# A ring of five 4 KB cells in place of seven, value loads in single cells, and two more resident rows of wq

## The chip, the cores and the metric

One core of one Trainium2 chip. The time is the device time of one execution in microseconds; a kernel's runs are compared with runs of the kernel before taken in the same rounds on the same chip. Lower is better. The sets of runs were taken on different chips; where two kernels of different sets are compared by their medians below, the difference by their ratios is the same within 4 us.

PE is the engine of the matmuls, DVE, ACT and POOL are the vector, scalar and GpSimd engines, and SP is the engine whose queue issues all loads. A load *lands* when the last of its 16 completion increments has come.

## The reference, cut to what matters

A decode step of two layers. Both layers use the same weights and the same key and value cache.

```python
B, Sq, D = 8, 1, 512; Hq, Hkv, Sk, Dh = 32, 8, 8192, 128; F = 1792      # bfloat16
for layer in range(2):
    x = x + attention(layernorm(x), k_cache, v_cache, wq, wo)    # softmax(q k^T * Dh**-0.5) v, then wo
    x = x + silu(layernorm(x) @ w1) @ w2
```

The cache is 134 MB of keys and 134 MB of values. Keys are read once and serve both layers, values are read once for each layer: in all 134 + 268 MB, and with them 38 MB of wo, 21 MB of wq and 4 MB of FFN weights.

## The kernel before

A small planner in the program, run when it is built, replays an estimated timetable of loads and engine work. It fixes the order of instructions on every engine and the cell that each load goes to. All loads stand in one queue (SP), in one order. Keys have eight slots of their own. Values, wo tiles and the rows of the second half of wq share a ring of cells of 4 KB a partition (512 KB a cell); a load waits until PE has read what its cell held before.

```python
N_CELL = 7
class Plan:
    PE_SLOW = 1.15                         # factor on the estimates of PE's work
    @staticmethod
    def place(free, cells):                # which cell: a lone free one for one cell, two side by side for a pair
        ...
def values(h, wo=None, cells=2):           # one unit: one batch, one KV head, one layer
    for P in range(4):                     # four quarters of the values
        if P == (2 if cells == 2 else 3) and wo is not None:
            h["wo"] = load_wo(wo)          # layer 0 only: its wo tile, ahead of the unit's last value load
        if P % cells == 0:
            vn = load_v(b, g, P, cells)
        def pv(P=P, vn=vn): ...            # 8 matmuls read the cell
        n = plan.add(f"v{u}.{P}", "PE", 0.35, pv, pr, [h["exp"], vn, old or clear_n] + vs[-1:])
        if P % cells == cells - 1:
            frees(n, vn)                   # only now may the cells be loaded again
    ...                                    # gather, spread, multiply by wo: only then is the wo cell free
def queries_1(tag, prio, b0, nb, deps):    # heads 16 to 31
    for kt in range(KT):                   # four rows of the second half of wq, through the ring, for every batch
        wn = load_wq(1, kt)
        ...
```

The batches go through in passes. A pass takes in eight keys and the values that go with them (the *mixed stretch*), then a run of values and wo tiles without keys (the *value-only stretch*), then the FFN and the next pass.

Of the kernel before, what the change touches and what calls it, by code (L numbers as in the profile page):

```python
# [8 lines left out]
DH = 128  # L9
SM_SCALE = DH ** -0.5  # L10
LN_EPS = 1e-5

N_CELL = 7
N_SC = 3
N_P = 3
N_DEF = 4
# [119 lines left out]
class Plan:  # L136
# [3 lines left out]
    RATE = {1: 2.57, 2: 2.51, 4: 2.48}  # L140
    LAND = 2.0
    HOP = 0.1
    PE_SLOW = 1.15

    def __init__(self):
        self.nodes = []
# [104 lines left out]
def _build(ctx, nc, A_x, A_k_cache, A_v_cache, A_wq, A_wo, B_w1, B_w2, out):  # L251
# [9 lines left out]
    GR = SLOT // 4  # L261
# [5 lines left out]
    def sb(shape, dt, name):  # L267
        return ctx.enter_context(nc.sbuf_tensor(name, shape, dt))
# [4 lines left out]
    ring = sb([128, N_CELL * GR], BF16, "ring")  # L273
    kts = sb([128, G * SLOT], BF16, "kts")
    wq0 = sb([128, KT, GR], BF16, "wq0")
    w1_sb = sb([128, KT, F], BF16, "w1")
    w2_sb = sb([128, FT, D], BF16, "w2")
    ident = sb([128, 128], BF16, "ident")
# [38 lines left out]
    syn = Sync(nc, ctx)  # L317
    ksem = [DmaCounter(syn.new_sem(f"kt{i}")) for i in range(G)]
    rsem = [DmaCounter(syn.new_sem(f"ring{i}")) for i in range(N_CELL)]
    wsem = {n: DmaCounter(syn.new_sem(f"w_{n}")) for n in ("w1", "w2", "x", "wq0")}  # L320
    osem = syn.new_sem("osem")

    table = {}
# [331 lines left out]
    def queries_1(tag, prio, b0, nb, deps):  # L655

        qp = MI[:, 0:16 * nb]
        last = []
        for kt in range(KT):
            wn = load_wq(1, kt)  # L660

            def mul(kt=kt, wn=wn):
                steps = []
                for h in range(16):
                    steps.append(lambda h=h: pe.matmul(
                        qp[:, h * nb:(h + 1) * nb], gran(wn.give)[:, h * DH:(h + 1) * DH], xn[:, b0:b0 + nb, kt],
                        start=(kt == 0 and h == 0), stop=(kt == KT - 1), skip_group_check=True))
                mms(steps, reads=cells_of(wn) + [res("xn")], writes=[res("misc")], add=kt > 0)

            last = [plan.add(f"{tag}.r{kt}", "PE", 0.5, mul, prio, [wn] + deps + last)]  # L670
            frees(last[0], wn)
        n = plan.add(f"{tag}.qc4", "DVE", 0.17, lambda: query_copy(4, 8, qp, nb), prio, last)
        return {g: n for g in range(4, 8)}

# [23 lines left out]
    def keys(layer, b, g, q_dep, late=None, first=False):  # L698
# [39 lines left out]
        for q in range(4):  # L738
            def score(q=q):

                kv = slot(g).rearrange("p (c y i f) -> p y f c i", c=8, y=8, f=4)
                steps = []
                for y in range(2):
                    for t in range(4):
                        w = bd[:, 48 * q + 16 * (1 - y):48 * q + 16 * (1 - y) + 32]
                        steps.append(lambda t=t, y=y, w=w: pe.matmul(  # L746
                            sc[32 * t:32 * t + 32, 0:256], w, kv[:, 2 * t + y, q],
                            start=(q == 0 and y == 0), stop=(q == 3 and y == 1)))
                mms(steps, reads=[res("kt", g), res("bd", u % N_BD)], writes=[res(*scr)], add=(q > 0))
            sn.append(plan.add(f"s{u}.{q}", "PE", 0.3, score, pr - 1,  # L750
                               [tn[3], bn] + sn[-1:]))

        if layer == 1:
# [62 lines left out]
    ot_users = []  # L816
    es = []

    def values(h, wo=None, cells=2):

        layer, b, g, u, sm = h["layer"], h["b"], h["g"], h["u"], h["sm"]
        pr = count[0] - 1
        pt, o = ps[sm], len(ot_users) % N_OT
        ot = OT[o]
        hd = slice(R * g, R * g + R)
        old = back(ot_users, N_OT)
        vs = []
        for P in range(4):
            if P == (2 if cells == 2 else 3) and wo is not None:
                h["wo"] = load_wo(wo)  # L830
            if P % cells == 0:
                vn = load_v(b, g, P, cells)

            def pv(P=P, vn=vn):


                vt = gran(vn.give, cells).rearrange("p (a c t n) -> p a c t n", a=cells, c=2, t=4)[:, P % cells]
                steps = []
                for c in range(2):
                    for t in range(4):  # L840
                        k = 32 * (2 * P + c) + 8 * t
                        steps.append(lambda t=t, c=c, k=k: pe.matmul(  # L842
                            ot[32 * t:32 * t + 2 * R, 0:2 * DH], pt[:, k:k + 2 * R], vt[:, c, t],
                            start=(P == 0 and c == 0), stop=(P == 3 and c == 1)))
                mms(steps, reads=cells_of(vn) + [res("p", sm)], writes=[res("ot", o)], add=(P > 0))
            n = plan.add(f"v{u}.{P}", "PE", 0.35, pv, pr, [h["exp"], vn, old or clear_n] + vs[-1:])
            if P % cells == cells - 1:
                frees(n, vn)
            vs.append(n)

        def high():
            op(act, lambda: act.activation(pt[:, :], ot[:, 0:2 * DH], ACT.Copy), reads=[res("ot", o)],  # L852
               writes=[res("p", sm)])

        def low():
            op(dve, lambda: dve.tensor_tensor(part[:, :], ot[:, 0:2 * DH], pt[:, :], ALU.subtract),  # L856
               reads=[res("ot", o), res("p", sm)], writes=[res("part")])

        def gather():

            steps = []
            for k, src in enumerate((pt, part)):
                for y in range(2):
                    steps.append(lambda k=k, src=src, y=y: pe.matmul(  # L864
                        EX[:, 0:R], src[:, y * DH:y * DH + DH], diag[:, R * y:R * y + R],
                        start=(k == 0 and y == 0), stop=(k == 1 and y == 1)))
            mms(steps, reads=[res("p", sm), res("part"), res("diag")], writes=[res("ex")])

        hn = plan.add(f"hi{u}", "ACT", 0.42, high, pr - 2, [vs[-1]])
        ln = plan.add(f"lo{u}", "DVE", 0.45, low, pr - 2, [hn, back(es, 1)])  # L870
        es.append(plan.add(f"g{u}", "PE", 0.2, gather, pr - 2, [ln, back(ot_users, 1)]))
        if layer == 1:
            def norm():
                op(dve, lambda: dve.tensor_tensor(qab[:, b, hd], EX[:, 0:R], rcp[sm], ALU.mult),
                   reads=[res("ex"), res("rcp", sm)], writes=[res("attnb", g, b)])

            h["n"] = plan.add(f"n{u}", "DVE", 0.17, norm, pr - 2, [es[-1], h["rc"]])
        else:
            zt = zts[o]

            def cast():
                op(act, lambda: act.activation(attna[:, hd], EX[:, 0:R], ACT.Copy), reads=[res("ex")],
                   writes=[res("attna", g)])

            def spread():
                steps = [lambda j=j: pe.matmul(  # L886
                    EX[:, 8 + R * j:8 + R * j + R], sel[:, j].rearrange("p a k -> p (a k)"), attna[:, hd],
                    start=True, stop=True) for j in range(R)]
                mms(steps, reads=[res("sel"), res("attna", g)], writes=[res("ex")])

            def own():
                v = EX[:, 8:8 + R * R].rearrange("p (j h) -> p j h", h=R)
                op(dve, lambda: dve.tensor_tensor(  # L893
                    zt[:, :].rearrange("p (j h) -> p j h", h=R), v,
                    rcm[sm].unsqueeze(1).to_broadcast([128, R, R]), ALU.mult),
                    reads=[res("ex"), res("rcm", sm)], writes=[res("z", o)])

            n = plan.add(f"cast{u}", "ACT", 0.2, cast, pr - 2, [es[-1]])
            n = plan.add(f"spread{u}", "PE", 0.2, spread, pr - 2, [n])
            h["n"] = plan.add(f"own{u}", "DVE", 0.17, own, pr - 2, [n, h["rc"]])  # L900
            h["z"] = o
        ot_users.append(h["n"])
        p_users[sm] = [vs[-1], h["n"]]
# [39 lines left out]
    free_yt = [None]  # L943
    y_now = [None]

    def a_values(h, cells=2):
        values(h, wo=h["g"], cells=cells)
        y_now[0] = out_proj_a(h, y_now[0] if h["g"] else free_yt[0])

    ffn_deps = []  # L950
# [46 lines left out]
    for b in range(-1, NB):  # L997
        ready = None
        prio = FIRST
        if b >= 0:  # L1000
# [3 lines left out]
            ready = norm_nodes(f"c{b}.ln2", prio, b, 1, [n])  # L1004
            second_q.update(queries_0(f"c{b}", prio, b, 1, [ready]))
            for h in held:
                values(h, cells=1)
                ends.append(h)
        ks, vs, held_units = pass_of(b)
        made = {}  # L1010
# [2 lines left out]
        def advance(unit):  # L1013
            while unit not in made:
                k = todo.pop(0)
                layer, kb, g = k
                if layer == 0:
# [2 lines left out]
                        load_wq0()  # L1020
                        first_q.update(queries_0("f", FIRST, 0, NB, [f5]))
                    if kb == 0 and g == 4:
                        first_q.update(queries_1("f", count[0] - 5, 0, NB, [f5]))
                    made[k] = keys(0, kb, g, first_q[g])
                else:
                    if g == 4:
                        second_q.update(queries_1(f"c{b}", count[0] - 3, b, 1, [ready]))
                    made[k] = keys(1, kb, g, second_q[g], held_units.index(k) if k in held_units else None, g == 0)

        for i, v in enumerate(vs):  # L1030
# [1 line left out]
            if b == NB - 1 and i == 5:  # L1032
                load_wo_all()
            if v[0] == 0:
                a_values(made[v], cells=1 if b >= 0 and i >= len(vs) - 3 else 2)
            else:
                values(made[v], cells=1 if i < 2 else 2)
                ends.append(made[v])
        held = [made[k] for k in held_units]
        if b < 0:  # L1040
# [69 lines left out]
```

## Time and profile before

| | before |
|---|---|
| median time, first measurement | 1188.71 us (1183.99 to 1195.29, 3 runs) |
| bytes read from HBM | 465.05 MB |
| busy: PE, DVE, ACT, POOL | 60%, 51%, 12%, 10% |
| share of the chain that ended last that is DMA | 76% |

It is a kernel bound by the stream from HBM: no engine is near full, and the DMA engines are busy from end to end. The views that carry this are in the prediction. Two more are wanted later. The first has time windows of the kernel before over one value-only stretch and the mixed stretch that follows; after the window and its length come busy time and instructions of PE, PE's weight loads, DVE, ACT and POOL, then the granted clock, the DMA share and GB/s.

```profile
224.00:265.00 41.00, 28.87 (x580) 14.70 (x584) 13.01 (x42) 4.55 (x16) 2.50 (x6) 0.54 1.02 406
266.00:363.00 97.00, 56.64 (x1056) 29.37 (x1048) 60.12 (x168) 12.30 (x43) 11.64 (x29) 0.74 1.01 413
```

Both stretches run at the rate of a full queue. The second has the waits of the queue's sequencer, SP (total us, times, longest):

```profile
SPq L91 <- PE ot L842: 654.1, 300, 21.5
SPq L91 <- PE sc L746: 155.1, 29, 13.2
SPq L91 <- PE yt L915: 28.6, 17, 3.7
```

SP waits most of the time for PE to release a cell (ot is the values' product, yt the product with wo). That costs nothing as long as enough issued loads still stand in the DMA queue.

### The profile page before, as it was taken

What the parts mean: (1) busy time and instruction counts of PE and PEld (TensorE: products, weight loads), DVE (VectorE), ACT (ScalarE), POOL (GpSimd) and SP (SyncE); (2) the same over time, 40 slices, a digit from 0 to 9 for tenths busy, and PEclk for the clock granted to TensorE, in tenths of its full rate; (3) what the DMA queues carried; (4) which work ended last, traced back from release to release, by engine and by line L of the source; (5) the groups of instructions that cost most, each with busy time, mean ns of one, the idle gap of its engine ahead of it and who ended that gap; (6) DMA issues with size and microseconds to landing.
All of it is one profiled execution on the core that took longest, in us unless ns stands there. A gap on an engine that the chain in (4) does not pass through costs nothing.

```text
span 1180.7 us, 31675 instructions
## 1 busy us (share of the span) xinstructions
PE 706.9 (60%) x13588; PEld 370.5 (31%) x13588; DVE 597.7 (51%) x1713; ACT 136.9 (12%) x475; POOL 117.3 (10%) x295
## 2 busy tenths in 40 slices
PE   2544555675565755666665755667556575566844
PEld 1322332242332423323332323324233242333423
DVE  5652367625564255733667254752557336663321
ACT  0010011101111110110111111111101111111110
POOL 1000011101110010100111010110001001110110
PEclk9765677657676676756777568765667567675775
DMA  9999799999999999999999999999999999999993
GB/s 365 421 419 346 311 420 421 414 403 403 422 411 412 398 381 417 422 408 391 421 421 407 400 412 412 415 411 400 413 415 406 371 393 421 422 410 403 384 354 149
DMA packets 86413, 467.13 MB, mean 396 GB/s; under 512 B 8944, under 2 KB 14848, under 8 KB 61952
## 3 DMA queue, kind: packets, MB, share of 16 engines
q1 hardware_dynamic: 86272, 465.10, 97.8%
q8 instruction: 107, 1.75, 0.6%
q14 instruction: 34, 0.28, 0.1%
HBM read 465.05 MB, written 0.01 MB: 394 GB/s over the span
## 4 chain that ended last, share of the span: by engine, by line
DMA 76%; PE 16%; issue 4%; DVE 2%; SPq 1%; POOLq 0%; ACT 0%; POOL 0%; DVEq 0%; ACTq 0%
DMA ring<-in_A_v_cache_dram 70%; PE ot L842 7%; PE sc L746 6%; DMA kts<-in_A_k_cache_dram 3%; DMA ring<-in_A_wq_dram 2%; DMA w<-in_B_w_dram 1%; DVE kts L694 1%; PE misc L642 1%; SPq L340 1%; PE ex L864 0%; PE sc L721 0%; PE yt L915 0%; PE misc L510 0%; DVE small L758 0%; PE ex L886 0%
## 5 line engine op out<-in xcount | busy, mean ns | idle before, releaser
L842 PE MATMUL ot<-ring,p 128*8 128x256 bf16 x4096 | 256.6, 365 | 220.8 <-DMA ring<-in_A_v_cache_dram 218.9
L694 DVE STREAM_TRANSPOSE kts<-kts 128x1024 uint32<-128x1024 uint32 x256 | 306.1, 1222 | 35.4 <-DMA kts<-in_A_k_cache_dram 35.3
L746 PE MATMUL sc<-kts,bd 128*32 128x256 bf16 x4096 | 288.6, 406 | 33.8 <-DVE kts L694 21.7
L842 PEld LDWEIGHTS ot<-ring,p 128*8 128x8 bf16 x4096 | 80.0, 92 | 313.9 <-DMA ring<-in_A_v_cache_dram 288.7
L746 PEld LDWEIGHTS sc<-kts,bd 128*32 128x32 bf16 x4096 | 116.3, 117 | 107.4 <-DVE kts L694 32.1
L856 DVE TENSOR_TENSOR part<-ot,p 128x256 bf16<-128x256 f32 x128 | 54.2, 423 | 177.1 <-ACT p L852 98.5
L763 POOL PARTITION_ALL_REDUCE small<-small x128 | 47.8, 373 | 637.4 <-DVE small L759 383.1
L772 ACT ACTIVATE expd<-sc,small 128x256 bf16<-128x256 f32 x128 | 60.7, 474 | 422.1 <-DVE small L767 365.6
L852 ACT ACTIVATE p<-ot 128x256 bf16<-128x256 f32 x128 | 49.1, 383 | 487.7 <-PE ot L842 486.7
L778 PE MATMUL sc<-expd,ident 128*32 128x256 bf16 x512 | 42.3, 318 | 91.1 <-ACT expd L772 88.4
L758 DVE TENSOR_REDUCE small<-sc 128x1 f32<-128x256 f32 x128 | 53.2, 415 | 51.3 <-PE sc L746 51.2
L792 POOL PARTITION_ALL_REDUCE small<-small x128 | 55.3, 432 | 214.2 <-DVE small L788 214.2
L729 DVE TENSOR_TENSOR bd<-sc,mask 128x64 bf16<-128x64 f32 x128 | 27.7, 217 | 83.1 <-PE sc L746 73.9
L785 DVE STREAM_TRANSPOSE p<-sc 128x256 bf16<-128x256 bf16 x128 | 56.9, 445 | 7.3 <-PE sc L778 4.5
L778 PEld LDWEIGHTS sc<-expd,ident 128*32 128x32 bf16 x512 | 15.4, 109 | 121.9 <-ACT expd L772 119.5
L788 DVE TENSOR_SCALAR small<-hm,small 128x4 f32<-128x4 f32 x128 | 26.4, 206 | 33.4 <-ACT expd L772 33.4
L864 PE MATMUL ex<-diag,p 128*128 128x4 bf16 x256 | 26.3, 172 | 23.5 <-DVE part L856 21.2
L915 PE MATMUL yt<-z,ring 128*128 128x4 bf16 x1024 | 36.1, 166 | 6.1 <-DVE z L893 4.5
L915 PEld LDWEIGHTS yt<-z,ring 128*128 128x128 bf16 x1024 | 31.2, 100 | 27.0 <-issue 26.8
L864 PEld LDWEIGHTS ex<-diag,p 128*128 128x128 bf16 x256 | 16.4, 104 | 72.2 <-issue 38.5
L767 DVE SCALAR_TENSOR_TENSOR small<-small,hm 128x4 f32<-128x4 f32 x128 | 19.4, 152 | 37.4 <-POOL small L763 37.2
L759 DVE TENSOR_SCALAR small<-hneg,small 128x4 f32<-128x4 f32 x128 | 29.4, 230 | 4.5
(82 smaller groups left out, 433.9 us busy)
## 6 DMA issues: line engine op xcount, KB each, us to landing
ring<-in_A_v_cache_dram SPq DMA_DIRECT2D x260, 512.0 KB, 8.2
kts<-in_A_k_cache_dram SPq DMA_DIRECT2D x64, 2048.0 KB, 11.2
ring<-in_A_v_cache_dram SPq DMA_DIRECT2D x126, 1024.0 KB, 11.0
ring<-in_A_wo_dram SPq DMA_DIRECT2D x64, 512.0 KB, 11.3
ring<-in_A_wq_dram SPq DMA_DIRECT2D x36, 512.0 KB, 9.7
kts<-in_A_wo_dram SPq DMA_DIRECT2D x2, 2048.0 KB, 15.8
w<-in_B_w_dram SPq DMA_DIRECT2D x2, 1792.0 KB, 13.2
wq<-in_A_wq_dram SPq DMA_DIRECT2D x4, 512.0 KB, 11.2
```

Of the source, the lines that this page charges most:

```text
L694: op(dve, lambda: dve.transpose(v, v), reads=[], writes=[res("kt", g)], add=(q > 0))
L746: steps.append(lambda t=t, y=y, w=w: pe.matmul(sc[32 * t:32 * t + 32, 0:256], w, kv[:, 2 * t + y, q], start=(q == 0 and y == 0), stop=(q = ...
L758: op(dve, lambda: dve.tensor_reduce(mxr[si], sv, AX.X, ALU.max), reads=[res(*scr)], writes=[res("mxr", si)])
L763: op(pool, lambda: pool.partition_all_reduce(mxa[si], mxp[si], 128, bass.bass_isa.ReduceOp.max), reads=[res("mxp", si)], writes=[res("mxa" ...
L772: op(act, lambda: act.activation(pe_out[:, :], sv, ACT.Exp, bias=bias[si], scale=SM_SCALE, accum_out=rsum[si]), reads=[res(*scr), res("bia ...
L778: steps = [lambda P=P: pe.matmul(sc[32 * P:32 * P + 32, 256:512], src[:, P], pe_out[:, :], start=True, stop=True) for P in range(4)]
L785: op(dve, lambda: dve.transpose(pt[:, :], src), reads=[res(*scr)], writes=[res("p", sm)])
L792: op(pool, lambda: pool.partition_all_reduce(ssa[si], ssm[si], 128, bass.bass_isa.ReduceOp.add), reads=[res("mxp", si)], writes=[res("mxa" ...
L842: steps.append(lambda t=t, c=c, k=k: pe.matmul(ot[32 * t:32 * t + 2 * R, 0:2 * DH], pt[:, k:k + 2 * R], vt[:, c, t], start=(P == 0 and c = ...
L852: op(act, lambda: act.activation(pt[:, :], ot[:, 0:2 * DH], ACT.Copy), reads=[res("ot", o)], writes=[res("p", sm)])
L856: op(dve, lambda: dve.tensor_tensor(part[:, :], ot[:, 0:2 * DH], pt[:, :], ALU.subtract), reads=[res("ot", o), res("p", sm)], writes=[res( ...
L915: steps.append(lambda j=j, dt=dt: pe.matmul(YT[:, dt * R:(dt + 1) * R], w[:, j, dt * 128:(dt + 1) * 128], zt[:, R * j:R * j + R], start=(g ...
```

## The change

Intent: 8 KB a partition are taken from the ring and hold two of the four rows of wq's second half, which are then read once instead of nine times (8.4 MB less). A shorter ring has little room for pairs, so all value loads go in single cells. The planner's PE estimates are set anew.

```diff
-N_CELL = 7
+N_CELL = 5
+N_ROW = 2
-    PE_SLOW = 1.15
+    PE_SLOW = 1.0
+    wq1 = sb([128, N_ROW, GR], BF16, "wq1")
 ...  # queries_1
-            wn = load_wq(1, kt)
+            if kt >= N_ROW:
+                wn = load_wq(1, kt)
+            elif nb > 1:
+                wn = plan.load(f"wq1r.{kt}", 1, lambda kt=kt: dma(sp, wq1[:, kt, :], ...), ring=False)
+            else:
+                wn = None
 ...
-            sn.append(plan.add(f"s{u}.{q}", "PE", 0.3, score, pr - 1,
+            sn.append(plan.add(f"s{u}.{q}", "PE", 0.45, score, pr - 1,
-    def values(h, wo=None, cells=2):
+    def values(h, wo=None, cells=1):
-            n = plan.add(f"v{u}.{P}", "PE", 0.35, pv, ...)
+            n = plan.add(f"v{u}.{P}", "PE", 0.4, pv, ...)
 ...  # callers no longer choose cells; queries of heads 16 to 31 also wait for those of heads 0 to 15
```

More of the change, by code (lines that the diff above doesn't have):

```diff
@@ L319, in _build @@
     rsem = [DmaCounter(syn.new_sem(f"ring{i}")) for i in range(N_CELL)]
-    wsem = {n: DmaCounter(syn.new_sem(f"w_{n}")) for n in ("w1", "w2", "x", "wq0")}
+    wsem = {n: DmaCounter(syn.new_sem(f"w_{n}")) for n in ("w1", "w2", "x", "wq0", "wq1")}
     osem = syn.new_sem("osem")
@@ L659, in queries_1 @@
         for kt in range(KT):
-            wn = load_wq(1, kt)
+            if kt >= N_ROW:
+                wn = load_wq(1, kt)
+            elif nb > 1:
+                wn = plan.load(f"wq1r.{kt}", 1, lambda kt=kt: dma(
+                    sp, wq1[:, kt, :], wq_v[:, kt, GR:2 * GR], wsem["wq1"], writes=[res("wq1")] if kt == 0 else (),
+                    adds=[res("wq1")] if kt else ()), ring=False)
+            else:
+                wn = None
             def mul(kt=kt, wn=wn):
+                w, held_in = (wq1[:, kt, :], [res("wq1")]) if kt < N_ROW else (gran(wn.give), cells_of(wn))
                 steps = []
@@ L665, in mul @@
                     steps.append(lambda h=h: pe.matmul(
-                        qp[:, h * nb:(h + 1) * nb], gran(wn.give)[:, h * DH:(h + 1) * DH], xn[:, b0:b0 + nb, kt],
+                        qp[:, h * nb:(h + 1) * nb], w[:, h * DH:(h + 1) * DH], xn[:, b0:b0 + nb, kt],
                         start=(kt == 0 and h == 0), stop=(kt == KT - 1), skip_group_check=True))
-                mms(steps, reads=cells_of(wn) + [res("xn")], writes=[res("misc")], add=kt > 0)
+                mms(steps, reads=held_in + [res("xn")], writes=[res("misc")], add=kt > 0)
             last = [plan.add(f"{tag}.r{kt}", "PE", 0.5, mul, prio, [wn] + deps + last)]
-            frees(last[0], wn)
+            if kt >= N_ROW:
+                frees(last[0], wn)
         n = plan.add(f"{tag}.qc4", "DVE", 0.17, lambda: query_copy(4, 8, qp, nb), prio, last)
@@ L845, in pv @@
                 mms(steps, reads=cells_of(vn) + [res("p", sm)], writes=[res("ot", o)], add=(P > 0))
-            n = plan.add(f"v{u}.{P}", "PE", 0.35, pv, pr, [h["exp"], vn, old or clear_n] + vs[-1:])
+            n = plan.add(f"v{u}.{P}", "PE", 0.4, pv, pr, [h["exp"], vn, old or clear_n] + vs[-1:])
             if P % cells == cells - 1:
@@ L944, in _build, with a_values @@
     y_now = [None]
-    def a_values(h, cells=2):
-        values(h, wo=h["g"], cells=cells)
+    def a_values(h):
+        values(h, wo=h["g"])
         y_now[0] = out_proj_a(h, y_now[0] if h["g"] else free_yt[0])
@@ L1006, in _build @@
             for h in held:
-                values(h, cells=1)
+                values(h)
                 ends.append(h)
@@ L1022, in advance @@
                     if kb == 0 and g == 4:
-                        first_q.update(queries_1("f", count[0] - 5, 0, NB, [f5]))
+                        first_q.update(queries_1("f", count[0] - 5, 0, NB, [f5, first_q[3]]))
                     made[k] = keys(0, kb, g, first_q[g])
@@ L1026, in advance @@
                     if g == 4:
-                        second_q.update(queries_1(f"c{b}", count[0] - 3, b, 1, [ready]))
+                        second_q.update(queries_1(f"c{b}", count[0] - 3, b, 1, [ready, second_q[3]]))
                     made[k] = keys(1, kb, g, second_q[g], held_units.index(k) if k in held_units else None, g == 0)
@@ L1034, in _build @@
             if v[0] == 0:
-                a_values(made[v], cells=1 if b >= 0 and i >= len(vs) - 3 else 2)
+                a_values(made[v])
             else:
-                values(made[v], cells=1 if i < 2 else 2)
+                values(made[v])
                 ends.append(made[v])
```

## The prediction

> **What bounds the kernel now.** I read the page first, its slices and its list of DMA issues. The kernel streams 465.05 MB from HBM into one core; everything else is small beside that.
>
> ```profile
> DMA  9999799999999999999999999999999999999993
> GB/s 365 421 419 346 311 420 421 414 403 403 422 411 412 398 381 417 422 408 391 421 421 407 400 412 412 415 411 400 413 415 406 371 393 421 422 410 403 384 354 149
> ...
> ring<-in_A_v_cache_dram SPq DMA_DIRECT2D x260, 512.0 KB, 8.2
> kts<-in_A_k_cache_dram SPq DMA_DIRECT2D x64, 2048.0 KB, 11.2
> ring<-in_A_v_cache_dram SPq DMA_DIRECT2D x126, 1024.0 KB, 11.0
> ring<-in_A_wo_dram SPq DMA_DIRECT2D x64, 512.0 KB, 11.3
> ring<-in_A_wq_dram SPq DMA_DIRECT2D x36, 512.0 KB, 9.7
> ```
>
> The DMA engines are busy in every slice but the fifth and the last, and what varies is the rate: 420 GB/s in good slices, about 400 in others. PE (60% busy), DVE (51%), ACT and POOL have room. So the bytes, and the rate at which full queues move them, set the time. A saving pays only if it removes bytes or an interval in which the queues run dry.
>
> Then I compared two stretches by time windows: 225 to 253 us, where only values and wo come in, all in 512 KB loads, and 163 to 225 us, where keys (2 MB) and paired values (1 MB) come too. The last three columns are the granted clock, the DMA share and GB/s.
>
> ```profile
> 225.00:253.00 28.00, 17.84 (x334) 7.92 (x334) 9.52 (x28) 2.98 (x11) 1.83 (x4) 0.56 1.03 406
> 163.00:225.00 62.00, 36.90 (x684) 19.75 (x684) 40.67 (x109) 7.97 (x29) 7.23 (x18) 0.72 1.01 419
> ```
>
> Both are saturated; small loads run some 3% slower. Last I read the chain of waits in the first of these, for the life of a ring cell:
>
> ```profile
> 234.18 7.39 DMA ring<-in_A_v_cache_dram
> 241.57 0.04 issue
> 241.62 0.63 PE ot L842 x7
> ...
> 242.31 8.17 DMA ring<-in_A_v_cache_dram
> 250.47 0.04 issue
> 250.52 0.63 PE ot L842 x8
> ...
> 251.21 8.59 DMA ring<-in_A_v_cache_dram
> ```
>
> A load lands, PE reads the cell in 0.63 us, and the next load into that cell goes out at once; from landing to the next issue is 0.7 us. The other 7.4 to 8.6 us are the load itself, most of it standing in a full queue. That queue is the reserve on which the change draws.
>
> **What the Trainium skill says.** "DMA: Bandwidth & Descriptors", section "Rules for kernel authors", asks for at least 1 MiB per DMA for most bandwidth. This trace agrees in sign only. With a full queue, from one load's last packet to the next one's, a 1 MB value load takes 2.53 us (median of 126) and a 512 KB one 1.288 us (of 260), so two halves cost 1.7% more, not the factor of a lone transfer. The same page, "Why small descriptors are slow", gives each packet a fixed overhead: the trace's packets of 4, 8 and 16 KB take 159, 309 and 612 ns (medians), which is about 9 ns plus 37.5 ns per KB. "SBUF — State Buffer", section "The DMA setup-cost knee", says each transfer has about 2 us that do not scale with bytes, mostly completion. Here a 512 KB load lands about 2.1 us after the mean of its engines has moved its last packet (part of that is the 16 engines' spread). A ring must cover this. "Perfetto Trace Analysis", section "Optimization Strategy", names the rival: repeated bubbles on the engine that should be saturated can mean too little SBUF for the next tile. In the trace before there are few: two gaps over 1 us near 125 to 128 us, none over 0.5 us elsewhere between start and tail.
>
> **The change, part by part.**
>
> *Two wq rows stay resident.* The second half of wq is read in four 512 KB rows, for the first layer and for each of 8 passes: the 36 loads above. After it, two rows are read once: 18 ring loads and 2 resident, 16 fewer. 16 x 0.524 MB = 8.39 MB, 1.8% of the bytes. All wq loads ran beside a full queue, so this is path time: 16 x 1.29 us = **-20.6 us**.
>
> *Value loads in single cells.* 126 loads of 1 MB become 252 of 512 KB. By load times: 126 x (2 x 1.288 - 2.532) = 5.5 us. By packets: each engine gets 16 packets instead of 8 for such a pair, 126 x 8 x 9 ns = 9 us. I take **+7 us**. 110 more issues of 0.33 us on SP (670 against 560) are hidden; SP mostly waits.
>
> *Five cells for seven.* The issue order of the two built programs tells, for every ring load, how many bytes stand between it and the previous tenant of its cell. Before, mostly 2.62 to 3.15 MB in stretches of values alone. After, 187 value loads have 2.10 MB (four loads) and 75 have 1.57 MB (three, because a wo tile holds a cell about 5 us); the 186 with 4.19 MB have a key load between and are safe. Is that enough? The shortest landing in the trace is 5.0 us, for a 1 MB load issued with 0.18 MB ahead of it; take off half its 2.5 us transfer, and a lone 512 KB load needs 3.75 us. With 0.04 + 0.63 + 0.1 us for PE and SP the least round of a cell is an estimated 4.5 us. Five cells at 1.285 us last 6.4 us, slack 1.9 us; four last 5.1 us, slack 0.6 us. So by itself the small ring still feeds the queues, just.
>
> What matters is delay of PE's reading beyond 0.64 us. Over the 260 single loads, landing to the end of PE's reading is 0.64 us at the median, 1.13 at the upper quartile, 2.5 at nine tenths. The long ones are at each pass boundary, where queries and scores go first:
>
> ```profile
> 259.84 0.60 PE L842 MATMUL ot<-ring,p 128*8 128x256 bf16 x8 [0.16 <-DMA ring<-in_A_v_cache_dram]
> 260.37 0.27 PE L721 MATMUL sc<-qtb,sel 128*128 128x4 bf16 x4
> 260.50 1.42 PE L642 MATMUL misc<-xn,wq 128*128 128x1 bf16 x48
> ...
> 263.82 0.62 PE L842 MATMUL ot<-ring,p 128*8 128x256 bf16 x8
> ```
>
> A cell landed at 261.1 us is read only by 264.4, 2.7 us late; seven cells absorb it, five have 1.9 us. The changed order puts one more query group (0.58 us) into that gap. Stall 0.8 to 1.4 us, at seven boundaries: **+8 us**. For the 75 loads on four cells I allow +3 us.
>
> *Back from pairs.* A pair of cells has to be free side by side, and is released only after both halves. Where that starved the queue before (slow loads near 93 to 101, 430 to 436 and 1122 to 1127 us, about 8 us above the medians together), single cells with 0.63 us of reading should recover half: **-4 us**. The planner's altered PE estimates only reorder PE; I give them nothing.
>
> Sum: -20.6 + 7 + 8 + 3 - 4 = about **-7 us**, on 1188.7: 1182. Being an adjustment of a tuned schedule whose estimates were evidently set again with it, I lean one us lower: **1181 us**.
>
> **Rivals.** (a) *Bytes alone decide.* If the queue stays full throughout, the sum is -20.6 + 7 - 4, near 1171; if the splitting is at its cheap end and all pair starvation goes, 1166. For it: the 4.5 us round against 6.4 us. Against it: the late reading at the boundaries, which is certain. (b) *The ring becomes the bound in value-only stretches.* 262 loads with 2.1 MB or less behind them; where the trace before had only 0.5 to 0.9 MB queued at an issue, 7 single loads took 1.75 us against 1.32. If half of the 262 paid 0.2 us, that is 26 us, and about 1205. Against it: those 7 loads came mostly in a stretch where one engine was slow by itself (landing 4 us after the mean's last packet), and leading engines' slack is not lost time. (c) *PE or DVE becomes the bound*: no; neither gets added work and PE waits for values in 218 cases, 218.9 us in all. (d) *The gap at the first pass boundary grows*: at 128 us the queue is empty because the next keys wait for scores of the second layer. Both orders place four single value loads after the weights and before that wait, so I expect the same gap, perhaps 2.5 us more.
>
> **Range and chances.** Eight in ten: 1166 (rival a in full) to 1198 (half of b). The medians of before spread 1184 to 1195, some of the width. Faster by over 2% needs under 1165, more than every byte saved plus every starvation ended: 0.06. Slower by over 2% needs over 1212, which is b at its worst: 0.06. Same: 0.88.
>
> **What would show it.** HBM bytes read 456.7 MB; value loads 512 x 512 KB with median issue to landing down from about 8 to 6 us in value-only stretches, while the rate there stays near 400 to 406 GB/s (right) or falls under 385 with DMA share under 0.97 (rival b). The last slices of each pass, once per about 140 us, should dip for some 1 us before the key load. If mixed stretches still show 419 GB/s, single loads cost less than 7 us; at 412 the packet sum is right. I am wrong if the DMA share falls in many slices, or if the time is under 1166, which would mean that pair loads and wq waits cost more than I saw.

## The result, and the profile after

| | before | after |
|---|---|---|
| median of 4 runs each | 1188.35 us (1183.99 to 1195.29) | 1255.07 us (1254.01 to 1260.82) |
| ratio | | 1.0566, 95% interval 1.0505 to 1.0626: slower |
| bytes read from HBM | 465.05 MB | 456.66 MB |
| rate over the span | 394 GB/s | 364 GB/s |

Ratios here and below are the mean time of one kernel's fast runs over that of the kernel before's fast runs of the same rounds, so not quite the ratio of the medians quoted. The time lies outside the predicted range of 1166 to 1198 us. All runs were fast.

The page of the kernel after, its slices and its DMA issues (KB each, median us from issue to landing):

```profile
DMA  9999799999999999999999999999999999999994
GB/s 364 401 412 343 295 391 409 353 323 383 382 401 345 327 389 400 409 319 365 376 392 404 317 367 373 416 370 334 381 380 414 354 336 403 404 415 316 335 369 170
...
ring<-in_A_v_cache_dram SPq DMA_DIRECT2D x512, 512.0 KB, 7.9
kts<-in_A_k_cache_dram SPq DMA_DIRECT2D x64, 2048.0 KB, 11.3
ring<-in_A_wo_dram SPq DMA_DIRECT2D x64, 512.0 KB, 9.5
ring<-in_A_wq_dram SPq DMA_DIRECT2D x18, 512.0 KB, 6.1
```

The bytes fell as meant. But once in every four or five slices the rate falls to between 316 and 336 GB/s, seven times over the run; before, there was no such comb. The DMA row still shows 9 there, so that row alone would have hidden it.

Time windows of the kernel after, over most of the same value-only stretch as above and the mixed stretch that follows:

```profile
230.00:279.00 49.00, 30.28 (x612) 15.60 (x616) 14.30 (x49) 4.84 (x17) 3.15 (x7) 0.54 0.92 327
282.00:382.00 100.00, 56.15 (x972) 24.57 (x964) 58.43 (x160) 11.68 (x40) 10.43 (x26) 0.69 0.99 389
```

The value-only window moves 16.0 MB in 49 us at 327 GB/s, where the window before moved 16.6 MB in 41 us at 406. The chain of waits in that stretch, kernel after:

```profile
248.89 6.71 DMA ring<-in_A_v_cache_dram
255.60 0.04 issue
255.65 0.63 PE ot L853 x8
...
256.33 5.41 DMA ring<-in_A_v_cache_dram
261.75 0.04 issue
261.79 0.60 PE ot L853 x8
262.39 1.58 PE misc L494 x56
...
264.69 6.46 DMA ring<-in_A_v_cache_dram
```

PE reads a cell in the same 0.6 us as before. The DMA pieces, 7.4 to 8.6 us before, are now 5.4 to 6.7 us: the loads stand less long in the queue, but two of the three are longer than the 5.6 us that five cells allow at the full rate (6.4 us less the 0.8 us that the prediction counts for reading and reissue). And SP's waits:

```profile
SPq L92 <- PE ot L853: 723.4, 475, 17.9
SPq L92 <- PE sc L757: 91.9, 29, 14.5
SPq L92 <- PE yt L926: 86.0, 40, 3.3
```

The waits for a cell that a wo tile holds (yt) have trebled, from 28.6 to 86.0 us.

To see where all of the time went I cut both traces by their DMA packets, pass by pass, for the six full passes in the middle. A *half* is 512 KB.

| mean of six passes | halves | us before | us after |
|---|---|---|---|
| value-only stretch | 35 | 46.4 | 56.0 |
| mixed stretch | 73 before, 71 after | 93.9 | 95.2 |

A pass grew by 9.6 + 1.3 us, six of them by 65 us; the start grew by 2 us and the last pass by some 6 us. That sums to the 73 us by which the two profiled runs are apart (1253.5 - 1180.7). Of the 1.3 us of the mixed stretch about half comes from one place alone, the gap at the first pass boundary, where the first key load was issued at 132.4 us instead of 128.7.

### The profile page after: what moved, and what is told of

It reads as the page before. It is cut to its first block, busy times and chain, and to the rows that moved or that the text cites. A ratio compares the mean times of both kernels' runs of the same rounds, so it can differ in the third digit from the quotient of the medians.

```text
span 1253.5 us, 31981 instructions
## 1 busy us (share of the span) xinstructions
PE 728.8 (58%) x13588; PEld 349.2 (28%) x13588; DVE 595.8 (48%) x1713; ACT 138.0 (11%) x475; POOL 117.2 (9%) x295
## 3 DMA queue, kind: packets, MB, share of 16 engines
q8 instruction: 107, 1.75, 0.5%
HBM read 456.66 MB, written 0.01 MB: 364 GB/s over the span
## 4 chain that ended last, share of the span: by engine, by line
DMA 69%; PE 20%; issue 5%; DVE 4%; ACT 1%; SPq 1%; POOL 0%; POOLq 0%; DVEq 0%; ACTq 0%
DMA ring<-in_A_v_cache_dram 61%; PE sc L757 7%; PE ot L853 7%; DMA ring<-in_A_wq_dram 5%; DMA kts<-in_A_k_cache_dram 2%; PE yt L926 1%; DMA w<-in_B_w_dram 1%; PE misc L644 1%; DVE kts L705 1%; PE ex L875 1%; PE ex L897 1%; PE sc L732 1%; PE misc L675 1%; DVE part L867 1%; ACT expd L783 0%
## 5 line engine op out<-in xcount | busy, mean ns | idle before, releaser
L853 PE MATMUL ot<-ring,p 128*8 128x256 bf16 x4096 | 273.0, 359 | 346.7 <-DMA ring<-in_A_v_cache_dram 343.3
L757 PE MATMUL sc<-kts,bd 128*32 128x256 bf16 x4096 | 294.3, 405 | 22.2 <-DVE kts L705 16.2
L853 PEld LDWEIGHTS ot<-ring,p 128*8 128x8 bf16 x4096 | 61.8, 85 | 477.0 <-DMA ring<-in_A_v_cache_dram 465.9
L757 PEld LDWEIGHTS sc<-kts,bd 128*32 128x32 bf16 x4096 | 111.2, 117 | 91.2 <-DVE kts L705 29.6
L789 PE MATMUL sc<-expd,ident 128*32 128x256 bf16 x512 | 44.9, 339 | 55.4 <-ACT expd L783 54.9
L904 DVE TENSOR_TENSOR z<-ex,rc 128x16 bf16<-128x16 f32 x64 | 11.1, 173 | 73.4 <-PE ex L897 73.4
L459 POOL TENSOR_TENSOR rstd<-var,expo 128x1 f32<-128x1 f32 (+1 forms) x17 | 10.9, 643 | 243.4 <-DVE var L449 212.2
```

The lines of the kernel that those rows point to most:

```text
L757: steps.append(lambda t=t, y=y, w=w: pe.matmul(sc[32 * t:32 * t + 32, 0:256], w, kv[:, 2 * t + y, q], start=(q == 0 and y == 0), stop=(q = ...
L789: steps = [lambda P=P: pe.matmul(sc[32 * P:32 * P + 32, 256:512], src[:, P], pe_out[:, :], start=True, stop=True) for P in range(4)]
L853: steps.append(lambda t=t, c=c, k=k: pe.matmul(ot[32 * t:32 * t + 2 * R, 0:2 * DH], pt[:, k:k + 2 * R], vt[:, c, t], start=(P == 0 and c = ...
```

## The experiments

Three theories were set against each other. Theory A: the five-cell ring is the cause; the time from the issue of a load to the next load into its cell, the *round*, is longer than five cells last. Theory B: the single loads, or PE's new order, are the cause. Theory C: the resident rows are. Theory W, later: within A, it is the wo tile's long hold of a cell.

### Seven cells, single loads, no rows

```diff
-N_CELL = 5
-N_ROW = 2
+N_CELL = 7
+N_ROW = 0
```

> The changed kernel with seven cells and no resident row of wq: what remains of the change is single value loads and the planner's new PE estimates (465.06 MB as before). Theory A (five cells are too few for the time that one load takes to come round): the loss goes; 1185 to 1197 us, that is before plus 0 to 9 us for splitting 126 loads, and 400 GB/s or more in the value-only stretches. Theory B (the single loads themselves or the new order on PE cost the time, the ring does not): 1260 to 1275 us, since 8.4 MB more are read than in the changed kernel.

1182.8 us (1182.28 to 1183.54), ratio 0.9988 (0.9966 to 1.0011). The whole loss is gone. A time window over its value-only stretch:

```profile
226.00:262.00 36.00, 25.94 (x528) 13.30 (x532) 9.39 (x34) 3.59 (x13) 1.95 (x4) 0.55 1.03 409
```

Theory B falls: single loads and the new estimates together neither cost nor gain over 0.4%.

### Five cells, no rows

```diff
-N_ROW = 2
+N_ROW = 0
```

> The changed kernel with its five cells and no resident row, so that all four rows of wq go through the ring as before. Theory A: slower than the changed kernel by the 16 loads that come back, 16 x 1.3 to 1.75 us = 21 to 28 us, 1276 to 1283 us; and 80 us or more over the same kernel with seven cells. Theory C (the resident rows, by their place in PE's order, do the harm): near 1190 us.

1280.19 us (1275.48 to 1287.23), ratio 1.0805 (1.0747 to 1.0863). Theory C falls: the rows are worth 1280.2 - 1255.1 = 25 us on the five-cell ring (28 by the ratios). Between five and seven cells, all else equal, are 1280.2 - 1182.8 = 97 us.

### Seven cells and two rows that are never loaded

The two rows are read from the held rows of the first half. The result is wrong by construction (the comparison's tolerance did not notice it).

```diff
-N_CELL = 5
+N_CELL = 7
-    wq1 = sb([128, N_ROW, GR], BF16, "wq1")
+    wq1 = wq0
-            elif nb > 1:
-                wn = plan.load(f"wq1r.{kt}", ...)
```

> Seven cells, single value loads, and two rows of wq that are read from the rows of the first half already held, so never loaded; the result is wrong on purpose, since seven cells and two rows do not fit in SBUF together. 455.6 MB, 18 loads fewer than before. Theory A: the bytes pay in full when the ring is long: 18 x 1.29 = 23 us less than the seven-cell kernel without rows, 1163 to 1173 us. If the wq loads were hidden beside other limits: as the seven-cell kernel without rows, within 5 us.

1157.31 us (1156.12 to 1162.07), ratio 0.978 (0.9751 to 0.981). That is 25.5 us below the seven-cell kernel for 18 loads fewer, 1.42 us each. The intent of the change was sound and worth some 16 x 1.42 = 23 us; what paid for it was not.

### The former PE estimates on the changed kernel

```diff
-    PE_SLOW = 1.0
+    PE_SLOW = 1.15
-... "PE", 0.45, score   ... "PE", 0.4, pv
+... "PE", 0.3, score    ... "PE", 0.35, pv
```

> The changed kernel with the planner's former PE estimates (factor 1.15, 0.3 us a score quarter, 0.35 us a value quarter), so with another order on PE and nearly the same distances in the ring (75 loads with 1.57 MB between, 192 with 2.1 MB). Theory A: within 1% of the changed kernel, 1243 to 1268 us. Theory B in the form that PE's order holds cells too long: back to 1180 to 1200 us.

1255.92 us (1247.19 to 1258.19), ratio 1.0592 (1.0547 to 1.0637). No effect.

### The wo tile later in the queue

In the changed kernel, a wo tile stands in the queue just ahead of its unit's last value load. It can be used only after that load, its product and four more steps, and holds its cell all that time. Here it is queued one further value load behind its unit's last one, so two places later.

```diff
-            if P == (2 if cells == 2 else 3) and wo is not None:
-                h["wo"] = load_wo(wo)
             if P % cells == 0:
                 vn = load_v(b, g, P, cells)
+                for w in waiting: w[1] -= 1
+                while waiting and waiting[0][1] <= 0: plan.loads.append(waiting.pop(0)[0])
+            if P == 3 and wo is not None:
+                h["wo"] = load_wo(wo)
+                waiting.append([plan.loads.pop(), 1])
```

> The changed kernel (five cells, two rows), but each wo tile is put in the queue one value load behind its unit's last value load instead of one ahead of it, so that it lands just before it is read and holds its cell for some 2 us instead of 5 to 7; then no load has fewer than four others between it and the previous tenant. Theory W (the wo tile's long hold leaves four cells, and four can't cover a round): of the excess of the value-only stretches, some 7.4 us a pass in their first twenty loads go down to about 2; 1208 to 1225 us. Theory F (five cells are too few with or without wo): 1240 us or more.

1217.77 us (1211.69 to 1226.47), ratio 1.0281 (1.0218 to 1.0344): 37 us better (34 by the ratios). In value-only stretches the time from a wo tile's landing to the end of PE's reading fell from 7.1 us (13 tiles) to 1.2 us (21 tiles). Their rate rose, but not to 406:

```profile
232.00:272.00 40.00, 27.53 (x574) 14.89 (x571) 9.76 (x35) 3.98 (x14) 1.96 (x4) 0.54 0.98 361
```

So theory W holds for 34 to 37 us, and at least as much is left.

### Two cells for wo alone

```diff
-N_ROW = 2
+N_ROW = 0
-    wq1 = sb([128, N_ROW, GR], BF16, "wq1")
+    wob = [sb([128, GR], BF16, f"wob{i}") for i in range(2)]
-        return load_cells(f"wo{g}", 1, ...)
+        i = wo_count[0] % 2 ...            # load into wob[i] once its last user has read it
```

> Five cells for values and wq, two further cells for wo alone, no resident row: the same SBUF as the seven-cell kernel, but values can use only five of it. Theory W: values keep five cells throughout, so it loses only what five cells lose at the pass boundaries and a little on the way, 1205 to 1240 us against 1280 with five shared cells. Theory F: 1255 us or more.

1222.7 us (1214.62 to 1230.59), ratio 1.0316 (1.0245 to 1.0388). With as much SBUF as the seven-cell kernel it is 40 us slower than that: setting cells apart for wo keeps wo from harming values, and leaves values with only five. It is also 57 us better than five cells that values and wo share (1280.2), so wo's presence in the ring costs more than its long hold alone.

### Six cells and one row, with wo as it was and later

```diff
-N_CELL = 5
-N_ROW = 2
+N_CELL = 6
+N_ROW = 1
```

> Six cells and one resident row, otherwise the changed kernel. 67 loads have 2.1 MB between them and the previous tenant, 185 have 2.62 MB. Theory A with a threshold (a cell's round of about 6.5 us has to fit in the cells): near the seven-cell kernel less one row, 1172 to 1195 us. If the loss were linear in cells (97 us between five and seven with no rows): 1183 + 48 - 12, near 1220 us.

1199.87 us (1194.23 to 1202.74), ratio 1.0123 (1.0065 to 1.018). This lies between the two ranges that were expected: the loss is not linear in cells and is mostly gone at six, but not wholly. Then the same with wo one value load behind its unit's last:

> Six cells, one row, and wo one value load later: no load has less than 2.62 MB between it and the previous tenant, as in the kernel before. Theories A and W together: the full worth of one row, 8 loads of 1.3 to 1.4 us less than the seven-cell kernel (1182.8), so 1168 to 1176 us, about 1% faster than before. If six cells still starve at the boundaries: 1176 to 1190 us.

1205.51 us (1199.45 to 1208.34), ratio 1.0165 (1.0114 to 1.0215). A miss. In the value-only stretches it did help (49.8 us for 35 halves became 49.4 for 36), but the mixed stretch went from 93.6 us for 72 halves to 94.7 for 71. Most of that is the first of the six, 97.3 us that became 106.8: the first pass's last wo tile now stood behind the two FFN weight loads and landed at 118.7 us instead of 105.9. The FFN waits for its product, and so do the scores that free the next key slot; the first key load of the next pass was issued at 133.4 us instead of 126.4. SP's longest wait for scores grew from 13.7 to 21.2 us. In the other five, 92.8 us for 72 halves became 92.2 for 71, at 1.28 us a half a loss of some 0.7 us: around one wo tile near the end of the keys, a value load and a key load came late. Later is not better everywhere.

### Values always on four cells

One cell of the five for wo alone, four for values and wq, two rows.

```diff
-N_CELL = 5
+N_CELL = 4
+    wob = [sb([128, GR], BF16, "wob0")]   # and as above, with one cell
```

> Two resident rows and five cells as in the changed kernel, but one of the five takes wo alone and values always have exactly four. This measures a cell's round. If the round were the 4.5 us that the prediction worked out, four cells (5.1 us at full rate) would still feed the queue: a load every 1.29 us in the value-only stretches, 1200 to 1225 us. If the round is the 6.2 to 7.9 us that the traces since show, a load comes every 1.55 to 1.95 us there: some 260 loads x 0.27 to 0.65 us more, 1250 to 1330 us.

1307.45 us (1306.93 to 1317.16), ratio 1.1053 (1.1011 to 1.1095). The measurement is not clean, because the one wo cell is itself waited for (SP waits of this kernel):

```profile
SPq L92 <- PE ot L863: 606.2, 399, 16.2
SPq L92 <- PE yt L936: 243.5, 41, 7.6
```

Away from the wo tiles (nine value loads in each of seven passes, from a little after the third wo tile on) a load came every 1.65 us (1.285 us and a mean excess of 0.36). Four of them are a round of 6.6 us, not 4.5.

### Values first at the pass boundary, on five, six and seven cells

```diff
-            pr = prio + 2 * (g0 > 0)                  # later query groups
+            pr = prio if g0 == 0 or nb > 1 else count[0]
-        pr = FIRST + 4 if first else u                # first scores of a pass
+        pr = u
```

On five cells with two rows, and with wo one value load behind its unit's last:

> The five-cell kernel with wo one load later, and at the pass boundary the values' matmuls go ahead of the later query groups and of the first scores. Theory L (the late reading on PE at the boundary makes the stall in the last ten loads of a pass, 3.3 us): about 2 us a pass less, 1198 to 1208 us against 1218. If those ten loads are slow for the ring's own reasons: 1213 us or more.

1215.64 us (1212.17 to 1220.42), ratio 1.0267 (1.0225 to 1.0308), against 1217.77: no difference that the runs can show. The 1198 to 1208 us that the late reading was expected to give did not come. The excess over 1.285 us a load in the last ten value loads of a pass did fall from 3.3 to 2.1 us, but some of it came back elsewhere. On six cells, one row and wo straight behind its unit's last value load (five rounds):

> Candidate: six cells, one row, wo straight behind its unit's last value load (not one further, which cost 2 us a pass where keys come in), and the values first at the boundary. If wo and late reading are what holds six cells back: the full worth of a row, 1168 to 1180 us, at or up to 1.5% below the kernel before. Otherwise as six cells without these, 1190 to 1203 us.

1179.78 us (1176.39 to 1183.73), ratio 0.9957 (0.9927 to 0.9988). This is 20 us better than six cells without the two remedies, and the last ten loads' excess fell from 1.9 to 0.6 us; what each remedy gave was not tested apart. It beats the kernel before by 0.4%, the only version with a right result that does so with an interval clear of 1 by more than a hair, and far less than the 2% that would count as faster here. On seven cells:

> Seven cells, single loads, no row, values first at the boundary. Theory L: the last ten loads of a pass have only 0.9 us of excess with seven cells, so at most 6 us less than 1182.8; 1176 to 1184 us. If delaying the first scores costs time by itself: 1186 us or more.

1182.21 us (1179.26 to 1183.38), ratio 0.9973 (0.9948 to 0.9999). With seven cells there was little to gain.

### The curve, and five cells with both remedies

```diff
-N_CELL = 5                     (six cells, no rows)
-N_ROW = 2
+N_CELL = 6
+N_ROW = 0
```

> Six cells, single loads, no resident row: the point between 1183 us (seven) and 1280 us (five) on one curve without bytes moving. Knee at a round of about 8 us (six cells cover 7.7 us, seven 9.0): 1200 to 1215 us. Straight line: 1230 us.

1208.64 us as the median of its three fast runs (1206.85 to 1216.57; a fourth, 1225.29, was slow, being 1.5% above the fastest at the same clock), ratio 1.0225 (1.017 to 1.028).

```diff
+N_CELL = 10                    (ten cells, no rows; wrong on purpose)
-    w2_sb = sb([128, FT, D], BF16, "w2")
+    w2_sb = w1_sb[:, :, :].rearrange("p k f -> p (k f)").rearrange("p (t d) -> p t d", d=D)   # and no load of w2
```

> Ten cells, single loads, no resident row; the room comes from laying the second FFN matrix over the first, whose load is then left out (1.8 MB, 5 us), so the result is wrong on purpose. Knee: seven cells are enough and three more bring only those 5 us, 1173 to 1181 us. Smooth curve: seven cells still starve in places (excess 21 us over the full rate in the value-only stretches), and ten bring 10 to 20 us more than the 5: 1158 to 1168 us.

1185.11 us (1184.09 to 1185.91), ratio 1.0006 (0.9968 to 1.0044). Three more cells bring nothing in total. It is 4 us more than the most that was expected with a knee, since this kernel loads 1.8 MB less: its value-only stretches did get 0.8 us shorter, but its mixed stretches took 96.4 us against 94.2 with seven cells, and no run says why. The rate of one value-only stretch of each, six and ten cells, in the order told:

```profile
227.00:267.00 40.00, 26.75 (x552) 13.98 (x556) 9.71 (x35) 3.98 (x14) 1.95 (x4) 0.54 0.99 378
```

```profile
224.00:259.00 35.00, 25.65 (x528) 13.27 (x532) 9.78 (x34) 3.60 (x13) 1.96 (x4) 0.55 1.03 408
```

| no rows, single loads | five | six | seven | ten |
|---|---|---|---|---|
| time, us | 1280 | 1209 | 1183 | 1185 |
| 35 halves of a value-only stretch, us | 56.6 | 49.7 | 47.0 | 46.2 |

For this kernel there is a knee at seven cells (3.7 MB): a step of 71 us, one of 26, then none. The second row of the table carries it better than the first; at the full rate of 1.285 us a half, 35 halves take 45.0 us.

Last, five cells and two rows with wo straight behind its unit's last value load and the values first at the boundary (the two edits above together, with a lag of 0):

> Five cells and two rows with wo straight behind its unit's last value load and the values first at the boundary. If these two account for the loss beyond a fixed cost of about 0.2 us a load in value-only stretches (290 loads, 58 us): 1195 to 1215 us. If five cells free of long holds were enough, as the prediction had it: below 1180 us.

1220.93 us (1217.86 to 1225.36), ratio 1.0315 (1.0273 to 1.0356), above both ranges that were expected. Five cells with both long holds cut (a wo tile still stays 3.0 us from landing to the end of its reading, 18 tiles) are still some 60 us behind seven cells and two rows (1157.31, which also leaves out the two loads that happen once, 2 x 1.42 us).

## Why the prediction was wrong

**The bound.** Right: it is the stream, and only bytes and dry queues count. Both halves of that sentence showed, the bytes as a gain and the dry queue as a larger loss.

**Resident rows, -20.6 us.** Right in kind, a little small: 1.42 us a load with seven cells, so 23 us for 16, and 25 us measured on the five-cell ring.

**Single loads, +7 us, and back from pairs, -4 us.** The sum of the two was put at +3; measured, with the new estimates, it is a ratio of 0.9988 (0.9966 to 1.0011), so about -1 us and at most +1.3. The parts can't be told apart by these runs.

**The ring, +8 and +3 us.** Here it failed: the prediction gave the small ring 11 us, and 97 us lie between seven and five cells without rows. Two terms were wrong and one estimate under them, the step that failed first: that a round of 4.5 us fits into the 6.4 us of five cells, "so by itself the small ring still feeds the queues".

- *The least round of 4.5 us.* It was built on the single shortest landing of the trace. With it, five cells had 1.9 us of slack. In the value-only stretches of the trace after, from one load's issue to the next issue into that cell is 7.9 us on average (160 loads: 6.7 to landing, 1.0 to the end of the reading, 0.2 to the issue), with 4.6 loads issued meanwhile; before it was 9.2 us with 6.6 loads. The ring lost two cells and the round only 1.3 us, so the loads come further apart. That the wait for the bytes themselves is short was right: the eight single loads of the trace after that were issued with under 0.3 MB queued landed in 4.5 us on average, and the best in 3.8 (the prediction's 3.75). What was wrong was to take a queue that is not empty for a full one. Single loads of the trace after, by what was queued when they were issued, and the time from the last packet of the one before to its own:

| queued, MB | under 0.5 | 0.5 to 0.7 | 0.7 to 0.9 | 0.9 to 1.1 | 1.1 to 1.3 | 1.3 to 2 | over 2 |
|---|---|---|---|---|---|---|---|
| loads | 30 | 57 | 67 | 66 | 51 | 54 | 269 |
| us a load | 2.00 | 1.94 | 1.65 | 1.48 | 1.41 | 1.40 | 1.30 |

  In this trace the rate begins to fall with more than 1 MB still queued. This was in the trace before too, as the 7 loads of 1.75 us that the prediction names under rival (b) and then explains away. Its reason was a misreading: only three of them (issued at 936.3, 937.6 and 938.8 us) stand in the stretch that it blames. The other four are the last value loads of passes (264.5, 543.7, 821.3 and 962.8 us); they took 1.63 to 1.83 us, and landed 1.5 to 1.6 us after their last packet, where 2.0 is the median.
- *"A wo tile holds a cell about 5 us", +3 us.* The 5 us were read rightly from the trace before (5.3 us over 18 tiles of value-only stretches) and carried over unchanged; in the changed kernel it was 7.1 us, as the value load that it waits for comes late itself, and queueing the tile later was worth 34 to 37 us.
- *Late reading at the boundary, +8 us.* It is there, and with six cells the last ten loads of a pass got 1.3 us faster with both remedies; on five cells the total moved by 2 us, inside the noise.

Of the 97 us, then, 34 to 37 are shown to be the wo tiles' hold and some 2 the late reading; the rest, some 60 us, is what five cells cost with values, wo and wq passing through them. Part of that is still the room that wo takes: with wo in two cells of its own, five cells were 40 us behind seven.

**Rival (b)** was what happened, at more than its size: the prediction gave it 26 us. The sign that it set for (b), under 385 GB/s and a DMA share under 0.97 in value-only stretches, is what the trace shows: 327 GB/s and 0.92. **Rival (d)** came true as well, at 3.7 us (the first key load after the first pass, 128.7 us before and 132.4 after) where it expected 2.5.

**What stays open.** Why a queue with 0.7 MB in it runs at three quarters of the rate. The records fit two readings. One: the 16 completion increments of a load are spread over 2.6 us (median, trace after; 2.7 before), and 2.6 us at 410 GB/s are 1.1 MB. A load counts as landed only with its slowest engine, so with less than that queued the fastest engines have nothing left while the slowest still work. In the stretch 240 to 270 us of the trace after, 81 of 2368 packets of 4 KB took over 400 ns (159 at the median, up to 2.0 us), against 11 of 2768 in 225 to 253 us before. But the records do not say which engine a packet ran on, and no run here levels the engines, so this is argued, not shown. The other: after the empty queue at 128.7 us some 2 us passed from the issue until 16 packets were under way, and 2 us at 410 GB/s are 0.8 MB (an estimate from these two numbers), so with less queued than that a load comes too late for some engines whatever the spread of the earlier one. No run tells the two apart. Instruction fetches, which occupy one engine for 1 us each, 107 times, explain little of it: value-only loads of the trace after took 1.71 us within 4 us after one and 1.64 us otherwise.

## What to carry to other kernels

Shrinking a ring of buffers in a stream-bound kernel is not free down to the best-case round of one buffer. Take the bytes that stand queued at an issue from the trace, subtract what the change takes away, and ask what loads with so little queued cost already; where the trace has only a few such loads, believe them. And count a buffer that is loaded early and released late as missing from the ring for its whole stay, which grows when the ring starves.

## What the Trainium skill lacked or had wrong

- "DMA: Bandwidth & Descriptors", section "Rules for kernel authors" (at least 1 MiB per DMA for most bandwidth): behind a full queue the size made no net difference here. All 126 loads of 1 MB split in two gave a ratio of 0.9988, with the new planner estimates and without the wait for two cells side by side. What mattered is how much is queued, for which no page has a figure: 3.7 MB of ring were enough, 2.6 MB cost 8%.
- "Perfetto Trace Analysis", section "DMA Engine Tracks" (slices show actual busy time, without idle time): the DMA share fell from 1.02 to 0.92 in the value-only stretch while the rate fell from 406 to 327 GB/s. Packets of 4 KB were recorded with up to 2.0 us where 0.16 is normal (their mean rose from 164 to 183 ns), so the busy share hid about half of this starvation.
- "DMA: Bandwidth & Descriptors", section "Latency and other measured facts" (HWDGE first byte about 600 ns): after an empty queue (issue at 128.7 us, kernel before) the first packet began 0.97 us after the issue, and only some 2 us after it were 16 packets under way. The page has no figure for this spread over the engines, which counts when a load must land on all 16.
- "SBUF — State Buffer", section "The DMA setup-cost knee" (about 2 us fixed, mostly completion): a 512 KB load behind an almost empty queue took 4.5 us to land on average (8 loads). Of this 1.3 us is the transfer at the full rate, and 0.5 us the 0.2 MB that were still ahead on average; some 2.7 us remain, and 2.2 us in the fastest of the eight. The page's figure is near the best case and short of the average.
